# Three token blocks of 512 walked to and fro, and one addition of layer 1 done by accumulating DMAs

## The chip, the cores and the metric

The kernel runs on one core of one Trainium2 chip. The metric is the device time of one execution in microseconds. The kernel before takes 701.39 us (median of 3 runs, 701.15 to 702.93). TensorE (PE) multiplies; VectorE (DVE), ScalarE (ACT) and GpSimd (POOL) do the elementwise work; SyncE (SP) issues the DMAs.

## The reference

An attention block feeds two MLP layers, all in float32:

```python
scores = (1/8) * q @ k.T            # 2 batches, 8 heads, 768 positions, head_dim 64
keep   = (key < n_sink) | ((0 <= row - key) & (row - key < window))   # 4 sinks, window 128
x = softmax(scores where keep) @ v  # -> 1536 tokens x 512
h = x @ w_in                        # layer 1: 512 -> 2048
P = a0 + a1*h + a2*h^2 + a3*h^3
Q = 1 + |b0|*|h| + |b1|*h^2
x = (P / Q) @ w_out                 # 2048 -> 512
h = x @ w_in2                       # layer 2
out = (h * sigmoid(1.702*h)) @ w_out2
```

## The kernel before

**Tiling.** The 1536 tokens are cut into blocks (`TB`, line 31): 256, 384, 384 and 512 tokens, that is 2, 3, 3 and 4 query blocks of 128. The 2048 hidden columns are 16 tiles f of 128, in two halves of 8. A *unit* is one layer, one block and one half; `UNITS` (line 35) lists them layer by layer, half by half, block by block, so 8 units a layer. Every unit's result for a block is added to a partial sum `xf` that waits in SBUF until the block's second half comes.

**A piece.** Each unit is cut into pieces of up to 512 moving columns: one f for a block of 384 or 512 tokens, two f for the block of 256. A piece is a first product `h` (`g1`), the elementwise part (`el_a`, `el_b`) and a second product into `acc` (`g2`), which follows `LAG` = 3 pieces later. Every float32 factor is split into a high and a low float32r part, so each product is three matmuls: high x high, high x low, low x high. `g1` takes 4 row chunks x 3 = 12 matmuls for each f and block; `g2` in layer 1 takes 12 as well, with the block's tokens moving; `g2` in layer 2 takes 3 for each f and 128 tokens, with 512 weight columns moving.

**Elementwise, layer 1.** ACT writes `y` = |b0 h|, `z` (the square term, called sq) and `s`; DVE forms `s*h`, then `(s + a1)*h`, then `z = z + y` (line 713). ACT takes `r` = Ln(z), then Exp. DVE forms `gh` (the quotient), a correction in two steps (`z`, `s`), and `gl`, the low part. So DVE has seven operations a piece and ACT five. Layer 2 has two of each.

**Weights.** Every weight tile is loaded as int64 bits (`wraw`) and decoded once: ACT `dy`; DVE `dy`, `dt` and twice `dt<-wraw,dt`; then the high part (`wi` or `wo`, by ACT, DVE or POOL, whichever the planner picks), and the low part by DVE. There are 8 slots for each kind of weights, one more once attention is over, so a half's tiles can be decoded only as the half before it sets slots free.

**Attention** is done block by block: scores (PE, from `k` and `q`), masking with a running minimum `nm` (DVE `m`), Exp (ACT `a`), scaling by `rs` (`a<-a,rs`, POOL or DVE), transposes by `ident` (PE), copies `th` and `sT`, and the product with `vr` (PE). Layer 1 of a block needs all 8 heads of that block. While the first block's attention runs, PE gets filler matmuls (`acc<-zero`).

**What sets the order.** All operations are recorded and then ordered by a planner (`Program.play`): a list scheduler that prices every operation, picks the one with the longest tail plus a bias per category (`BIAS`), spaces the head pairs of attention (`HEAD`) and may hand an operation that several engines can do to another engine (`THETA`). Each engine then runs its list in exactly that order: an instruction that waits holds everything behind it on its engine. The profile gives the two lines of the planner's runner (L209 for matmuls and memsets, L210 for all else) for nearly all instructions, so groups are told apart by tile names.

The names in the steps that follow: pieces are counted from 0 in layer 1; `UNITS` (L35), `decode` (L605 on), `el_a`, `el_b`, `finish`, `attention`.

Of the kernel before, what the change touches and what calls it, by code (L numbers as in the profile page):

```python
# [6 lines left out]
F32R = mybir.dt.float32r  # L7
I32 = mybir.dt.int32
U32 = mybir.dt.uint32
AF = mybir.ActivationFunctionType  # L10
ALU = mybir.AluOpType
# [16 lines left out]
LN2_64 = 64.0 * 0.6931471805599453  # L28


TB = [[(0, [0, 1])], [(0, [2, 3, 4])], [(0, [5]), (1, [0, 1])], [(1, [2, 3, 4, 5])]]
XF_EARLY = (0, 1)

HALVES = [list(range(NF // 2)), list(range(NF // 2, NF))]
UNITS = [(m, T, fs) for m in (0, 1) for fs in HALVES for T in range(len(TB))]  # L35
GROUP = 3
LAG = 3

# [7 lines left out]
TH, SN, PE_OUT = "act/dve", "pool/dve", "act/dve"  # L46

BIAS = {
# [3 lines left out]
}  # L52
HEAD = (0.46, 1.43, 4.3, 7.1)
THETA = 1.27

WARM, FILL, FILL_AHEAD = 20, 6000, 0.1

# [4 lines left out]

START, PE_START, TICK, TICK_COLUMNS = 5.75, 6.25, 10.24 / 3, 3060
PE_LAT = 0.2
COL_FIX, COL_EACH = 0.4, 0.0275
TABLE = 1.3
LAT = 0.16
DMA_LAT, DMA_RATE, DMA_MIN = 1.9, 0.36e6, 65536


class View:
# [66 lines left out]
class Program:  # L138
# [56 lines left out]
    def op(self, eng, meth, alloc=(), alts=(), given=False, calls=(), cost=0.0, **kw):  # L195


        o = Op()
        o.i, o.eng, o.own = len(self.ops), eng, eng
        o.cat = self.cat  # L200
        o.table = 2 if kw.get("func") == AF.Sigmoid else 1 if kw.get("func") in (AF.Exp, AF.Ln) else 0
        views = [(k, v) for c in calls or [kw] for k, v in c.items() if isinstance(v, View)]

        def runner(eng, meth, kw):
            def run():
                a = {k: v.real() if isinstance(v, View) else v for k, v in kw.items()}
                e = getattr(self.nc, eng)
                if meth in ("matmul", "memset"):
                    return getattr(e, meth)(a.pop("out"), **a)  # L209
                return getattr(e, meth)(**a)  # L210
            return run
        o.lat = LAT
        o.nbytes = o.columns = 0
        if calls:
            runs = [runner(eng, meth, c) for c in calls]
            o.alts = {eng: (cost, lambda: [f() for f in runs][-1])}
            o.cost, o.lat = cost, PE_LAT
            o.columns = sum(c["rhs"].n * 4 * (c["lhsT"].box[0][1] - c["lhsT"].box[0][0]) / P for c in calls)
        elif eng == "sync":
            v = views[0][1]  # L220
            o.nbytes = (v.box[0][1] - v.box[0][0]) * v.n * 4
            o.cost, o.lat = 0.45 if v.box[0][1] - v.box[0][0] == P else 0.62, DMA_LAT
            o.alts = {eng: (o.cost, runner(eng, meth, kw))}
        else:
            self.columns = 0
            o.alts = {e: (self.price(e, m_, k_), runner(e, m_, k_)) for e, m_, k_ in [(eng, meth, kw)] + list(alts)}
            o.cost = min(c for c, _ in o.alts.values())
            o.columns = self.columns
            if eng == "tensor":
                o.lat = PE_LAT  # L230
        if given:
            o.alts, o.cost, o.lat, o.nbytes = {eng: (1e-6, lambda: None)}, 1e-6, given * 1.25 - 0.75, 0
        pre = {}
        for k, v in views:
            w = k in ("out", "accum_out")
            for q, box, wr in v.t.acc:
                if (w or wr) and overlap(box, v.box):
                    pre[q.i] = q
            if not v.t.acc:
                assert w, (v.t.name, k)  # L240
        o.allocs = [v.t for k, v in views if not v.t.acc] + [v.t for v in alloc if not v.t.acc]
        o.allocs = list(dict.fromkeys(o.allocs))
        o.begun = []
        for t in o.allocs:
            t.first = o
            t.acc.append((o, ((0, 0),), False))
        for t in dict.fromkeys([v.t for _, v in views] + [v.t for v in alloc]):
            if t not in o.allocs and not any(v.t is t for _, v in views):
                t.acc.append((o, ((0, 0),), False))
            if t.first is not o and t.first.i not in pre and (t.first.i, 0) not in pre:  # L250
                t.first.begun.append(o)
                pre[t.first.i, 0] = None
        for k, v in views:
            v.t.acc.append((o, v.box, k in ("out", "accum_out")))
        o.tiles = list(dict.fromkeys([v.t for _, v in views] + [v.t for v in alloc]))
        o.banks = [t for t in o.tiles if t.tag in PSUM_TAGS]
        o.preds = len(pre)
        o.succ = []
        o.next = []
        for q in pre.values():  # L260
            if q is not None:
                q.succ.append(o)
        o.ready = 0.0
        self.ops.append(o)
        return o
# [227 lines left out]
def emit(tc, qT, kX, vL, w_in, w_out, ca, cb, nw, out):  # L493
# [33 lines left out]
    def lo(eng, o, i, h):  # L527
        return tt(eng, ALU.subtract, o, i, h.bitcast(F32))

    cst_p = tc.tile_pool(name="cst", bufs=1)  # L530
    cst = cst_p.__enter__()
    SW = 2 * P + SC
# [72 lines left out]
    def decode(w, raw, dp, eng):  # L605

        lw, hw = raw[:, :, 0], raw[:, :, 1]
        y = R.tile(dp, [P, 512], F32, tag="dy", name="dy", bufs=2)
        t = R.tile(dp, [P, 512], I32, tag="dt", name="dt", bufs=2)
        R.op("scalar", "activation", out=y, in_=hw.bitcast(F32), func=AF.Abs)  # L610
        kw = dict(out=y, in0=y, scalar1=W_MIN, scalar2=W_MAX, op0=ALU.max, op1=ALU.min)
        R.op("vector", "tensor_scalar", **kw)
        kw = dict(out=t, in0=y.bitcast(I32), scalar1=0x07FFFFFF, scalar2=3, op0=ALU.bitwise_and, op1=ALU.logical_shift_left)
        R.op("vector", "tensor_scalar", **kw)
        R.op("vector", "scalar_tensor_tensor", out=t, in0=lw, scalar=29, in1=t, op0=ALU.logical_shift_right, op1=ALU.bitwise_or)
        R.op("vector", "scalar_tensor_tensor", out=t, in0=hw, scalar=-0x40000000, in1=t, op0=ALU.bitwise_and, op1=ALU.bitwise_or)
        hi(WH, w[:, 0, :], t.bitcast(F32))
        lo(eng, w[:, 1, :], t.bitcast(F32), w[:, 0, :])

    def moe(pools, blocks, units, x1_ready, late_pool):  # L620
# [80 lines left out]
        def el_a(i):  # L701
            m = steps[i][1]
            h = h_t.pop(i)[:, :wid(i)]
            if m == 0:
                y = R.tile(tp, [P, 512], F32, tag="y", name="y", bufs=2, more=(get_late, None, EL_MORE))[:, :wid(i)]
                s1 = R.tile(tp, [P, 512], F32, tag="s", name="s", bufs=2, more=(get_late, None, EL_MORE))[:, :wid(i)]
                z = R.tile(tp, [P, 512], F32, tag="z", name="z", bufs=2, more=(get_late, None, EL_MORE))[:, :wid(i)]
                R.op("scalar", "activation", out=y, in_=h, func=AF.Abs, scale=ab[:, 0:1])
                R.op("scalar", "activation", out=z, in_=h, func=AF.Square, scale=sb[:, 3:4])
                affine("act", s1, h, a_t[:, 3:4], a_t[:, 2:3])  # L710
                tt("dve", ALU.mult, s1, s1, h)
                R.op("vector", "scalar_tensor_tensor", out=s1, in0=s1, scalar=a_t[:, 1:2], in1=h, op0=ALU.add, op1=ALU.mult)
                tt("dve", ALU.add, z, z, y)
                el[i] = (z, s1)
            else:
                g = R.tile(tp, [P, 512], F32, tag="y", name="g", bufs=2, more=(get_late, None, EL_MORE))[:, :wid(i)]
                R.op("scalar", "activation", out=g, in_=h, func=AF.Sigmoid, scale=1.702)
                R.op("vector", "tensor_tensor", out=g, in0=g, in1=h, op=ALU.mult)
                el[i] = (g,)
# [108 lines left out]
    def build_banded():  # L828
        with (
# [22 lines left out]
            def attention(T, xs, alone):  # L852
# [74 lines left out]
                def scores(h):  # L927
# [9 lines left out]
                    for i, (b, qb) in enumerate(qs):  # L937
                        off, w = (P + SC, P) if qb == 0 else (0, 2 * P + SC)
                        k0 = kcol[b, max(0, qb - 1)] * KW
                        ps_ = [pst("s") for _ in t]  # L940
                        R.op("tensor", "matmul", alloc=[x for y in t for x in y[1:]], cost=w / 600 + 2 * COL_EACH, calls=[
                            dict(out=p[:, :w], lhsT=qr[r, i * P:(i + 1) * P], rhs=kr[r, k0:k0 + w], start=True, stop=True)
                            for p, (r, _, _, _) in zip(ps_, t)])
                        for p, (_, a, nm, sm) in zip(ps_, t):
# [48 lines left out]
                def values(h):  # L993
# [14 lines left out]
                    if sq:  # L1008
                        for e in (h, h + 1):
                            q0, n = qcol[sq[0]] * P, len(sq) * P  # L1010
                            calls.append(dict(out=x[(e % 2) * D:(e % 2 + 1) * D, q0:q0 + n], lhsT=vrs[e % 2][:SC, vcol[sq[0][0], "s"], :], rhs=st.pop(("sT", e))[:, :n], start=False, stop=True))
                    cost = COL_FIX + sum(c["rhs"].n / 1200 + COL_EACH for c in calls)
                    R.op("tensor", "matmul", calls=calls, cost=cost)
                    n, c = nq * P, h // 2
                    hi(XH, xs[0][c][:, :n], x[:, :n])
# [163 lines left out]
```

## Time and profile before

| what | value |
|---|---|
| median of 3 runs | 701.39 us |
| the profiled execution | 701.9 us |
| its span, first to last instruction | 700.1 us |
| PE busy | 670.2 us (96%) |
| DVE busy | 533.3 us (76%) |
| ACT busy | 407.2 us (58%) |
| POOL busy | 73.2 us (10%) |
| mean granted TensorE clock | 0.985 |

Busy shares are averages over the whole span. The 40-slice view shows DVE at 9 tenths in most slices up to about 420 us and at 1 to 8 tenths behind them, while PE stands at 9 nearly throughout. PE is pipelined: the mean time of one matmul is longer than the step from one to the next, which the chain of waits gives.

### The profile page before, as it was taken

How to read it: one execution, taken by the hardware profiler on the slowest of the kernel's cores; microseconds unless marked ns; L12 is line 12 of the kernel's file. 1: busy time of each engine (PE TensorE's matmuls, PEld its weight loads, DVE VectorE, ACT ScalarE, POOL GpSimd, SP SyncE). 2: the span in 40 equal slices, each digit the busy share in tenths (PEclk: the TensorE clock that was granted, in tenths of full speed). 3: DMA queues.
4: the chain of work that ended last, by engine and by line, in shares of the span. 5: the costliest groups of instructions: out<-in, count | busy, mean ns of one | idle time of the engine just before them, and what ended most of it. 6: DMA issues, size and time to landing. Idle time of an engine off the chain costs nothing.

```text
span 700.1 us, 10401 instructions
## 1 busy us (share of the span) xinstructions
PE 670.2 (96%) x3690; PEld 569.8 (81%) x3690; DVE 533.3 (76%) x1182; ACT 407.2 (58%) x894; POOL 73.2 (10%) x131
## 2 busy tenths in 40 slices
PE   8999989999999986799998999999999999999995
PEld 7677767877888865699997888988888898888874
DVE  7999899868759999999999999985278753222341
ACT  5899888967788665768585773543345432221220
POOL 4262452422200000000000000000000000000000
PEclk9999999999999997999999999999999999999999
DMA  5653554400001033300201011342023200000021
GB/s 170 212 171 109 157 156 137 154 26 1 24 0 31 31 118 111 106 27 8 84 0 32 1 58 63 121 141 70 1 91 120 91 31 16 0 16 1 15 76 65
DMA packets 26412, 49.75 MB, mean 71 GB/s; under 512 B 6384, under 2 KB 15088, under 8 KB 26352
## 3 DMA queue, kind: packets, MB, share of 16 engines
q1 hardware_dynamic: 26064, 49.00, 22.7%
q8 instruction: 31, 0.51, 0.3%
q14 instruction: 29, 0.24, 0.1%
q10 hardware_dynamic: 288, 0.00, 0.0%
HBM read 45.85 MB, written 3.15 MB: 70 GB/s over the span
## 4 chain that ended last, share of the span: by engine, by line
PE 82%; DVE 11%; ACT 3%; issue 1%; DMA 1%; POOL 1%; SPq 0%; DVEq 0%; POOLq 0%; ACTq 0%
PE att L209 32%; PE acc L209 25%; PE h L209 20%; PE att L210 3%; DVE dt L210 2%; DVE s L210 2%; DVE z L210 2%; PE acc L844 1%; DVE gh L210 1%; POOL a L210 1%; DVE dy L210 1%; DMA q<-q_t 1%; DVE wi L210 1%; DVE gl L210 1%; DVE m L210 1%
## 5 line engine op out<-in xcount | busy, mean ns | idle before, releaser
L209 PE MATMUL h<-xh,wi 128*128 128x384 f32 (+2 forms) x608 | 168.7, 342 | 7.2 <-DVE s L210 7.2
L209 PEld LDWEIGHTS h<-xh,wi 128*128 128x128 f32 x608 | 110.3, 193 | 21.7 <-DVE s L210 9.4
L209 PE MATMUL att<-xh,wi 128*128 128x384 f32 (+2 forms) x416 | 116.7, 343 | 0.6 <-DVE s L210 0.6
L209 PE MATMUL acc<-gh,wo 128*128 128x384 f32 (+2 forms) x384 | 105.7, 342 | 0.0
L209 PE MATMUL h<-xl,wi 128*128 128x384 f32 (+2 forms) x304 | 102.8, 338 | 0.0
L210 DVE TENSOR_TENSOR gl<-y,gh 128x384 fp32r<-128x384 f32 (+1 forms) x56 | 33.8, 613 | 82.1 <-PE acc L209 41.3
L209 PE MATMUL acc<-wo,gh 128*128 128x512 f32 x288 | 93.7, 395 | 0.0
L210 DVE SCALAR_TENSOR_TENSOR dt<-wraw,dt 128x512 int32<-128x512 int32 x128 | 89.0, 696 | 0.6
L209 PEld LDWEIGHTS att<-xh,wi 128*128 128x128 f32 x416 | 75.2, 188 | 7.6 <-DVE s L210 0.9
L210 ACT ACTIVATE gh<-y 128x384 fp32r<-128x384 f32 (+1 forms) x56 | 31.5, 569 | 75.9 <-PE acc L209 39.7
L209 PEld LDWEIGHTS acc<-gh,wo 128*128 128x128 f32 x384 | 69.2, 192 | 5.8 <-issue 2.0
L209 PE MATMUL att<-xl,wi 128*128 128x384 f32 (+2 forms) x208 | 71.4, 343 | 0.0
L210 POOL TENSOR_SCALAR a<-a,rs 128x272 f32<-128x272 f32 (+1 forms) x92 | 58.0, 647 | 109.2 <-DVE rs L210 71.8
L209 PE MATMUL acc<-gl,wo 128*128 128x384 f32 (+2 forms) x192 | 62.9, 341 | 5.9 <-DVE gl L210 5.9
L209 PEld LDWEIGHTS acc<-wo,gh 128*128 128x128 f32 x288 | 53.3, 188 | 10.4 <-ACT xf L210 0.4
L209 PEld LDWEIGHTS h<-xl,wi 128*128 128x128 f32 x304 | 58.7, 193 | 3.4 <-issue 0.4
L210 ACT ACTIVATE dy<-wraw 128x512 f32<-128x512 f32 x64 | 42.9, 670 | 25.8 <-DMA wraw<-w_out 14.1
L209 PE MATMUL acc<-wo,gl 128*128 128x512 f32 x144 | 52.7, 394 | 0.0
L210 ACT ACTIVATE a<-m,nm 128x272 f32<-128x272 f32 (+1 forms) x96 | 47.2, 493 | 5.5 <-DVE nm L210 4.7
L210 ACT ACTIVATE r<-z,ln_b 128x384 f32<-128x384 f32 (+1 forms) x56 | 37.0, 660 | 16.0 <-DVE z L210 15.8
L209 PEld LDWEIGHTS acc<-gl,wo 128*128 128x128 f32 x192 | 36.2, 192 | 10.1 <-DVE gl L210 7.8
L209 PE MATMUL att<-gh,wo 128*128 128x512 f32 (+2 forms) x128 | 40.8, 359 | 1.2 <-ACT xf L210 1.2
(118 smaller groups left out, 1234.4 us busy)
## 6 DMA issues: line engine op xcount, KB each, us to landing
wraw<-w_in SPq DMA_DIRECT2D x32, 512.0 KB, 3.6
wraw<-w_out SPq DMA_DIRECT2D x32, 512.0 KB, 3.5
out<-xf SPq DMA_DIRECT2D x12, 256.0 KB, 2.3
k<-k_x SPq DMA_DIRECT2D x12, 144.0 KB, 2.7
vr<-v_l SPq DMA_DIRECT2D x24, 64.0 KB, 2.5
k<-k_x SPq DMA_DIRECT2D x4, 360.0 KB, 3.6
vr<-v_l SPq DMA_DIRECT2D x8, 160.0 KB, 2.5
k<-k_x SPq DMA_DIRECT2D x4, 288.0 KB, 4.4
```

Source lines behind the costliest of these rows:

```text
L209: return getattr(e, meth)(a.pop("out"), **a)
L210: return getattr(e, meth)(**a)
L844: nc.tensor.matmul(R.real[k][:, 0:256], lhsT=zero[:, :P], rhs=zero, start=True, stop=True)
```

## The change

There are now three blocks of 512 tokens: batch 0's query blocks 0 to 3; its 4 and 5 with batch 1's 0 and 1; batch 1's 2 to 5. A piece is always one f and 512 columns: 48 pieces a layer, where there were 56 in layer 1 and 56 in layer 2. The units go to and fro: in layer 1 block 0 and block 1 with half 0, block 2 with both halves, block 1 and block 0 with half 1; in layer 2 block 2 and block 1 with half 0, block 0 with both halves, block 1 and block 2 with half 1. The block with both halves has no partial sum. In layer 1 `z = z + y` is a DMA from `y` to `z` that accumulates, issued by POOL. `dt` has three buffers, the planner's prices are new, and so are its tables (`BIAS`, `HEAD`, `THETA`). `add_minus` is defined and not called.

```diff
-TB = [[(0, [0, 1])], [(0, [2, 3, 4])], [(0, [5]), (1, [0, 1])], [(1, [2, 3, 4, 5])]]
-XF_EARLY = (0, 1)
+TB = [[(0, [0, 1, 2, 3])], [(0, [4, 5]), (1, [0, 1])], [(1, [2, 3, 4, 5])]]
+XF_EARLY = (0,)
-UNITS = [(m, T, fs) for m in (0, 1) for fs in HALVES for T in range(len(TB))]
+LAST = len(TB) - 1
+THERE, BACK = list(range(LAST)), list(range(LAST - 1, -1, -1))
+UNITS = ([(0, T, HALVES[0]) for T in THERE] + [(0, LAST, HALVES[0] + HALVES[1])] + [(0, T, HALVES[1]) for T in BACK]
+         + [(1, T, HALVES[0]) for T in [LAST] + BACK[:-1]] + [(1, 0, HALVES[0] + HALVES[1])] + [(1, T, HALVES[1]) for T in THERE[1:] + [LAST]])
...
-    "at0": 15.33, "at1": 21.93, "at2": 26.03, "at3": 6.7, "m0": -10.71, "m1": -2.77, "m2": -0.5,
+    "at0": 57.37, "at1": 40.94, "at2": -26.39, "at3": -86.3, "m0": -5.97, "m1": 87.68, "m2": 11.75,
...
-HEAD = (0.46, 1.43, 4.3, 7.1)
-THETA = 1.27
+HEAD = (5.08, 0.16, 15.06, 0.34)
+THETA = -0.68
...
-        elif eng == "sync":
+        elif meth == "dma_start":
...
+            if eng == "gpsimd":
+                o.nbytes *= 2
+                o.cost, o.lat = ADD_FIX, ADD_LAT + 0.6 * (kw["out"].dtype == F32R)
...
+    def add(out, in_):
+
+        R.op("gpsimd", "dma_start", out=out, in_=in_, accum_op=ALU.add)
...
-        t = R.tile(dp, [P, 512], I32, tag="dt", name="dt", bufs=2)
+        t = R.tile(dp, [P, 512], I32, tag="dt", name="dt", bufs=3)
...
-                tt("dve", ALU.add, z, z, y)
+                add(z, y)
```

**Where the first MLP matmul stands on PE.** `k,q` are scores, `th,vr` and `sT,vr` the products with v, `acc<-zero` fillers, `xh,wi` and `xl,wi` the first piece's `g1`. Before:

```order
L209 MATMUL h_324<-th_315,vr_200 64x256
L209 MATMUL h_324<-th_315,vr_200 64x128
L209 MATMUL att_294<-k_60,q_61 128x272
L209 MATMUL att_275<-k_60,q_61 128x272
L844 MATMUL acc_187<-zero 128x256 x5
L209 MATMUL att_322<-k_181,q_184 128x272
L209 MATMUL att_294<-k_181,q_184 128x272
L844 MATMUL acc_187<-zero 128x256
L209 MATMUL h_324<-xh_0_0_340,wi_302 128x256
L209 MATMUL h_324<-xl_0_0_348,wi_302 128x256
```

And of the change:

```order
L215 MATMUL h_432<-sT_386,vr_194 64x256
L215 MATMUL h_432<-sT_411,vr_198 64x256
L215 MATMUL att_359<-k_60,q_61 128x272
L215 MATMUL att_353<-k_60,q_61 128x272
L863 MATMUL acc_187<-zero 128x256 x6
L215 MATMUL h_432<-xh_0_0_459,wi_275 128x512
L215 MATMUL h_432<-xl_0_0_467,wi_275 128x512
L215 MATMUL att_357<-k_60,q_61 128x128
L215 MATMUL att_359<-k_60,q_61 128x128
```

Ahead of this row PE has 26 of the 96 score rows, 24 of 200 transposes, 16 of 144 products with v and 71 fillers before; of the change it has 40 of 96, 64 of 200, 40 of 136 and 130. Before its 25th MLP matmul the change has 56 scores, 96 transposes, 64 products and 153 fillers; the kernel before has as many scores, transposes and products (56, 92, 66) ahead of its 145th MLP matmul, with 110 fillers.

**ACT around the Ln of layer 1**, in the middle of the layer. `y`, `z`, `s` read the first product from PSUM (`h` or `att`), `r<-z` is the Ln, `r<-r` the Exp, `dy` and `wi` belong to the decoding. Before (the block of 512, first half):

```order
L210 ACTIVATE y_787<-h_324,ab 128x512
L210 ACTIVATE z_2341<-h_324,sb_179 128x512
L210 ACTIVATE r_691<-z_647,ln_b 128x512
L210 ACTIVATE s_2348<-h_324,a_t 128x512
L210 ACTIVATE dy_221<-wraw_64 128x512
L210 ACTIVATE wi_546<-dt_298 128x512
L210 ACTIVATE r_691<-r_691,ln_b 128x512
L210 ACTIVATE dy_243<-wraw_65 128x512
L210 ACTIVATE wi_611<-dt_239 128x512
L210 ACTIVATE y_2369<-att_275,ab 128x512
L210 ACTIVATE r_2358<-z_2341,ln_b 128x512
```

And of the change (block 2, both halves):

```order
L216 ACTIVATE y_933<-h_432,ab 128x512
L216 ACTIVATE z_961<-h_432,sb_179 128x512
L216 ACTIVATE s_976<-h_432,a_t 128x512
L216 ACTIVATE y_1062<-att_353,ab 128x512
L216 ACTIVATE z_2214<-att_353,sb_179 128x512
L216 ACTIVATE s_2219<-att_353,a_t 128x512
L216 ACTIVATE r_1001<-z_961,ln_b 128x512
L216 ACTIVATE r_1001<-r_1001,ln_b 128x512
L216 ACTIVATE r_2262<-z_2214,ln_b 128x512
L216 ACTIVATE r_2262<-r_2262,ln_b 128x512
L216 ACTIVATE dy_218<-wraw_64 128x512
```

Pieces now go through ACT in pairs, and each Ln, which waits for the accumulating DMA into its `z`, stands four instructions behind the one that wrote that `z`.

**Who does what.** Over the whole program, `a<-a,rs` on 272 columns stands 76 times on POOL and 4 times on DVE before, and 40 times on each of the change. The copies `th`, `sT` and `as` stand 3 times on DVE before and 38 times of the change. The high parts of the weights stand 6 times on POOL before and 27 times of the change, where POOL also issues the 48 DMAs.

## Rows read from the trace of the kernel before

**Rows 1.** The page's head and its busy times.

```profile
span 700.1 us, 10401 instructions
PE 670.2 (96%) x3690; PEld 569.8 (81%) x3690; DVE 533.3 (76%) x1182; ACT 407.2 (58%) x894; POOL 73.2 (10%) x131
```

**Rows 2.** Busy us by stretch: length, PE, PEld, DVE, ACT, POOL, clock, DMA.

```profile
36.00:91.00 55.00, 54.27 (x396) 41.66 (x395) 51.43 (x146) 49.65 (x149) 22.38 (x38) 1.00 0.49 141
91.00:212.00 121.00, 117.78 (x725) 95.29 (x724) 94.70 (x258) 94.75 (x253) 34.81 (x62) 0.99 0.23 69
212.00:300.00 88.00, 74.75 (x368) 63.58 (x367) 87.74 (x156) 59.97 (x100) 1.25 (x2) 0.93 0.27 84
300.00:410.00 110.00, 107.22 (x598) 100.64 (x598) 109.05 (x210) 77.49 (x136) 2.62 (x3) 1.00 0.07 20
410.00:693.00 283.00, 282.92 (x1400) 243.80 (x1398) 159.32 (x290) 100.12 (x184) 0.00 (x0) 1.00 0.18 56
```

**Rows 3.** Chain of waits, pieces from three windows: start, length, engine, tile, count.

```profile
283.84 0.42 DVE dt L210
...
284.86 0.60 DVE dt L210
...
293.54 0.66 DVE gh L210
...
484.87 2.08 PE att L209 x12
...
525.89 2.75 PE h L209 x12
...
556.76 2.87 PE h L209 x24
```

**Rows 4.** PE busy, 91 to 212 us, of tiles k, vr and ident in turn.

```profile
91.00:212.00 121.00, 14.11 (x80) 0.99 0.23 69
...
91.00:212.00 121.00, 24.67 (x156) 0.99 0.23 69
...
91.00:212.00 121.00, 18.01 (x108) 0.99 0.23 69
```

**Rows 5.** Groups by shape, DVE: name, shapes, count, busy us, mean ns, idle before.

```profile
L210 DVE TENSOR_TENSOR z<-z,y 128x384 f32<-128x384 f32 x32 | 18.3, 571 | 9.1 <-ACT z L210 9.1
...
L210 DVE TENSOR_TENSOR z<-z,y 128x512 f32<-128x512 f32 x24 | 16.3, 681 | 0.1
...
L210 DVE TENSOR_SCALAR a<-a,rs 128x272 f32<-128x272 f32 x4 | 1.6, 406 | 0.0
```

**Rows 6.** DMA issues: tiles, queue, count, KB each, median us to landing.

```profile
wraw<-w_in SPq DMA_DIRECT2D x32, 512.0 KB, 3.6
...
out<-xf SPq DMA_DIRECT2D x12, 256.0 KB, 2.3
...
q<-q_t SPq DMA_DIRECT2D x4, 192.0 KB, 4.5
```

**Rows 7.** Groups by shape, ACT on 512 columns.

```profile
L210 ACT ACTIVATE dy<-wraw 128x512 f32<-128x512 f32 x64 | 42.9, 670 | 25.8 <-DMA wraw<-w_out 14.1 <-DMA wraw<-w_in 11.6
...
L210 ACT ACTIVATE r<-r,ln_b 128x512 f32<-128x512 f32 x24 | 17.3, 721 | 0.4
...
L210 ACT ACTIVATE s<-h,a_t 128x512 f32<-128x512 f32 x15 | 11.6, 776 | 2.9 <-DVE gl L210 2.9
...
L210 ACT ACTIVATE y<-h,ab 128x512 f32<-128x512 f32 x15 | 10.3, 684 | 9.0 <-PE h L209 6.4 <-DVE dt L210 2.6
L210 ACT ACTIVATE z<-h,sb 128x512 f32<-128x512 f32 x15 | 10.2, 680 | 1.2 <-DVE s L210 1.2
```

**Rows 8.** Groups by shape, POOL.

```profile
L210 POOL TENSOR_SCALAR a<-a,rs 128x272 f32<-128x272 f32 x76 | 47.1, 635 | 76.7 <-DVE rs L210 44.6 <-ACT th L210 13.2 <-DVE nm L210 10.6
...
L598 POOL TENSOR_SCALAR mk<-mk 128x272 f32<-128x272 f32 x1 | 0.4, 419 | 0.2 <-DVE mk L596 0.2
```

**Rows 9.** Waits: engine, tile, releaser, us in total, times, longest.

```profile
POOL a L210 <- DVE rs L210: 71.8, 12, 21.1
```

More of the change, by code (lines that the diff above doesn't have):

```diff
@@ L64 @@
 PE_LAT = 0.2
-COL_FIX, COL_EACH = 0.4, 0.0275
+COL_EACH = 0.1
 TABLE = 1.3
@@ L68 @@
 DMA_LAT, DMA_RATE, DMA_MIN = 1.9, 0.36e6, 65536
+ADD_FIX, ADD_LAT = 0.9, 1.6
 class View:
@@ L528, in lo, with add_minus @@
         return tt(eng, ALU.subtract, o, i, h.bitcast(F32))
+    def add(out, in_):
+        R.op("gpsimd", "dma_start", out=out, in_=in_, accum_op=ALU.add)
+    def add_minus(o, i):
+        one_of([("gpsimd", "tensor_scalar", dict(out=o, in0=i, scalar1=-1.0, scalar2=0.0, op0=ALU.mult, op1=ALU.add)),
+                ("scalar", "activation", dict(out=o, in_=i, func=AF.Copy, scale=-1.0))])
+        add(o, i)
     cst_p = tc.tile_pool(name="cst", bufs=1)
@@ L940, in scores @@
                         ps_ = [pst("s") for _ in t]
-                        R.op("tensor", "matmul", alloc=[x for y in t for x in y[1:]], cost=w / 600 + 2 * COL_EACH, calls=[
+                        R.op("tensor", "matmul", alloc=[x for y in t for x in y[1:]], cost=w / 420 + 0.11, calls=[
                             dict(out=p[:, :w], lhsT=qr[r, i * P:(i + 1) * P], rhs=kr[r, k0:k0 + w], start=True, stop=True)
@@ L1011, in values @@
                             calls.append(dict(out=x[(e % 2) * D:(e % 2 + 1) * D, q0:q0 + n], lhsT=vrs[e % 2][:SC, vcol[sq[0][0], "s"], :], rhs=st.pop(("sT", e))[:, :n], start=False, stop=True))
-                    cost = COL_FIX + sum(c["rhs"].n / 1200 + COL_EACH for c in calls)
+                    cost = sum(c["rhs"].n / 1100 + COL_EACH for c in calls)
                     R.op("tensor", "matmul", calls=calls, cost=cost)
```

5 rows, old and new, of the table BIAS are left out of this document.

## The prediction

> **What bounds the kernel now.** The page's head gives the ratio of span to work: 700.1 us, PE busy for 96% of it, DVE for 76% [rows 1]. The profiled execution took 701.9 us, 1.8 more than its span and 0.5 more than the median of the runs shown; the sum below is made against the span, and these two are set right at the end. An average over the span hides which engine leads where, so the next view is busy time by stretch [rows 2]. From 36 to 91 us PE (54.3 of 55, part of it fillers) and DVE (51.4) are both near full. From 91 to 212 PE is full and DVE has room (94.7 of 121). From 212 to 410 DVE is full: 87.7 of 88 and 109.1 of 110, while PE loses 13.3 and 2.8 us and its clock falls to a mean of 0.93 in the first part. From 410 on PE alone is full.
>
> The step of one MLP matmul is read from the chain, where it is not blurred by pipelining [rows 3]: 2.87/24 = 0.1196 us with 256 columns, 2.08/12 = 0.1733 with 384, 2.75/12 = 0.2292 with 512. By the code there are 576, 1152 and 1152 of them, so 68.9 + 199.6 + 264.0 = 532.5 us.
>
> How much PE loses behind 91 us follows by subtraction. Ahead of that time stand, by the order, 144 MLP matmuls (132 with 256 columns, 12 with 384: 17.9 us), so 514.6 remain. Attention takes another 14.1 + 24.7 + 18.0 = 56.8 us there [rows 4]. That is 571.4 us of work in the 602 us up to 693: 30.6 are lost, 3.2 of them between 91 and 212. So the DVE-led stretch from 212 to 410 loses about 27 us, where the idle time alone shows 16; the rest is half clock and small gaps between matmuls.
>
> **The change, part by part.**
>
> *Fewer matmuls.* Three blocks of 512 need 2304 matmuls with 512 columns, 528.1 us instead of 532.5: −4.4. The columns are the same; only the fixed part of 576 matmuls goes. This lies on PE, which sets the end, so all of it counts.
>
> *The start.* Layer 1 can begin only when block 0's attention is through, and block 0 is now twice as large. I compare equal states. In the trace 80 of the 192 score records, two a row of the order, stand behind 91 us [rows 4]; so 56 of the 96 rows are done there, and 46% of the transposes. The changed order has the same ahead of its 25th MLP matmul, where the kernel before has done 144. At the same state, then, 17.9 − 24 × 0.2292 = 12.4 us of MLP work is missing. Is the state reached at the same time? DVE decides. Up to the second piece the order gives DVE as many decodes (14) as the kernel before has ahead of its fifth, about 3 pieces' elementwise work less (7 × 0.60 each, −12.6), 6 maskings less, 16 normalisations more (0.406 each [rows 5], +6.5) and 16 small copies more (no more than 0.42 each, a pass of DVE over 512 columns [rows 3], +5 to +7; the maskings at the same 0.42, −2.5). Net −2 to −4, and ACT and the fillers give nothing back, so the state comes at 91 to 95 us. I take +14; the bounds are +5 (PE picks matmuls up while it would have filled) and +22 (DVE waits on the longer chain of four score blocks a head).
>
> *The DVE-led stretch.* All 56 additions take 18.3 + 16.3 us by their own durations [rows 5]; at the chain's step, 0.60 where the mean of one is 0.68, some 30. About 36 of them lie between 212 and 410, 20 us. That leaves DVE 177 us of work there against 198 − 27 = 171 on PE: nearly even. The new order puts the heaviest part into block 2, which runs both halves at a stretch: 16 pieces and, by the order, 12 decodes. DVE needs 16 × (3 × 0.60 + 3 × 0.66) = 60.5 and 12 × (2 × 0.42 + 3 × 0.60) = 31.7, together 92.2 us; PE needs 16 × 24 × 0.2292 = 88.0. DVE leads by 4 there, and in the 16 pieces behind it (the way back, with few decodes) PE leads. So of 27 us some 21 come back. Bounds: 8, if DVE's heavier share of normalising (40 of 80 instead of 4) and copying is not done with when the stretch begins; 27, all of it.
>
> *The adds as DMAs.* POOL issues 48; what they cost is how long a Ln waits. ACT stands in order: behind a Ln that waits are the Exp of its piece, the next `y`, `z`, `s`, and so the PSUM banks of the next first products. The trace has no accumulating DMA. The nearest are 256 KB in 2.3 us and 512 KB in 3.6; the slowest is 4.5 [rows 6]. An accumulate reads two tiles of 256 KB and writes one, so I take 3.6, with bounds 2.3 and 4.5, plus what POOL is late. In the new order `s`, the next `y` and `z`, and `s` again stand between a `z` and its Ln: 0.776 + 0.684 + 0.680 + 0.776 = 2.9 us [rows 7]. A pair of pieces takes ACT 2 × (0.684 + 0.680 + 0.776 + 2 × 0.721) = 7.2 us and, with 18 decode steps and copies for block 2's 16 pieces at about 0.65, 8.6. PE needs 11.0 for a pair. So ACT can wait 2.4 us a pair, and an add costs nothing until it takes 2.9 + 2.4 = 5.3 us; each microsecond beyond costs 24 pairs × 1 = 24 us. At 3.6 the cost is 0. Below nothing it can't be: the Ln gets no earlier than after DVE's 0.68.
>
> GpSimd's own operations are slower beside a busy DVE: 0.635 us for 272 columns where the one on the quiet chip took 0.419 [rows 8]. The Trainium skill, page "SBUF — State Buffer", section "🔬 SBUF: two separate sides", has the rule behind it and against this change: GpSimd writes the descriptors of its DMAs through a port pair that a VectorE operation in a two-port mode holds for its whole length, so such DMAs wait. By that page's example (620 ns alone, about 3100 beside a copy) an add would take, as an estimate, 2.5 us more, and the sum would be some 19 us higher. I go by the row: 0.2 us a time, and 3.6 + 0.2 stays well under 5.3.
>
> *No cost taken:* the partial sums (one block fewer a layer, on ACT and DVE beside PE), the first units of layer 2 (they take block 2, whose input is ready long before), the end (four chunks of 512 as now).
>
> The sum: −4.4 + 14 − 21 + 0 = −11.4. From the profiled execution 701.9 − 11.4 = 690.5, less 0.5 to the median: 690 us.
>
> **Rivals.**
>
> *The adds are late.* Place: the Ln of layer 1 on ACT; it decides from 5.3 us on. For it: POOL is in order, and its queue in the attention phase waited 71.8 us in 12 waits for `rs`, 21.1 at the longest [rows 9]; an add behind such a normalisation waits as well, and rows 8 show POOL slowed by DVE. Against: no landing over 4.5 us, and behind attention POOL has only copies ahead of the adds. At 6.5 us an add, 1.2 × 24 = 29 us: 690 + 29 = 719. Slower.
>
> *The start takes what the stretch gives.* If the doubled first block costs 22 us and only 12 come back, −4.4 + 22 − 12 = +6; with the middle of either, 0. For it: DVE has 51.4 of 55 us filled in the start, and gets half of POOL's normalising. Against: equal work by the count above. About 701, no change that can be told.
>
> *All of it comes back.* If decodes spread evenly over layer 1 and the start costs 6: −4.4 + 6 − 27 = −25, 676 us. For it: DVE's total falls by more than PE's; against: the slots bind half 1's decodes to block 2.
>
> **How the numbers follow.** Forecast 0.46 (its own range 680 to 698), late adds 0.21, eaten by the start 0.16, all back 0.17. A measurement of this kernel tells about 0.3% (2 us) from no change. Faster are the forecast, the last case and a quarter of the third: 0.67; same 0.11; slower the late adds and a few of the third: 0.22. To leave 2 in 10 out, the range runs from 674, under the last case, to 707, the beginning of the late adds.
>
> **What would show it.** The first MLP matmul near 60 us instead of 36, and about 92 us at the 25th. PE idle between some 220 and 310 us down from 13 to under 5. DVE's total near 500 us. ACT's waits at `r<-z` for DMAs under 2.4 us a pair; if they come to more, and PE waits for ACT or for `gl`, the adds are late and the forecast is wrong. If PE is full from 91 us on and the time still is 700, the start was mis-sized.

## The result, and the profile after

The changed kernel takes 694.14 us (median of 4 runs, 693.83 to 695.05) where the kernel before took 701.27 (4 runs beside them): ratio 0.9891, 95% interval 0.9863 to 0.9918. That is 7.1 us less; 690 was predicted, within 674 to 707.

The page's head and its busy times, to be set against [rows 1]:

```profile
span 692.9 us, 9131 instructions
PE 670.3 (97%) x3141; PEld 518.0 (75%) x3141; DVE 518.8 (75%) x1101; ACT 380.0 (55%) x786; POOL 102.2 (15%) x144
```

PE's busy time is the same; the span is 7.2 us shorter. DVE lost 14.5 us, not the 34.6 of the additions. The stretches of [rows 2] (length, PE, PEld, DVE, ACT, POOL, clock, DMA):

```profile
36.00:91.00 55.00, 53.62 (x343) 37.15 (x342) 52.63 (x171) 43.07 (x131) 21.14 (x29) 1.00 0.63 179
91.00:212.00 121.00, 118.95 (x613) 83.31 (x611) 101.92 (x265) 90.36 (x223) 25.72 (x39) 1.00 0.37 88
212.00:300.00 88.00, 86.69 (x383) 68.15 (x382) 82.02 (x136) 59.44 (x98) 20.36 (x25) 1.00 0.42 89
300.00:410.00 110.00, 104.19 (x440) 82.82 (x440) 103.26 (x171) 73.99 (x117) 19.93 (x23) 0.98 0.42 92
410.00:693.00 283.00, 274.31 (x1190) 221.97 (x1188) 153.16 (x261) 93.66 (x159) 3.60 (x4) 0.99 0.20 60
```

From 212 to 300 us PE's idle time falls from 13.3 to 1.3 us and the clock is back at 1.00; from 300 to 410 it grows from 2.8 to 5.8. (1.00 is the upper of TensorE's two clock levels, 2.4 GHz; 0.50 would be the lower, 1.2 GHz; what lies between is a mean over both.) Where did the crowd of 260 to 300 go? DVE's busy time on the decoding tile `dt` alone, first the kernel before, then the changed one:

```profile
212.00:260.00 48.00, 13.97 (x23) 1.00 0.18 55
260.00:300.00 40.00, 19.31 (x33) 0.84 0.38 119
300.00:410.00 110.00, 9.75 (x16) 1.00 0.07 20
```

```profile
212.00:260.00 48.00, 13.17 (x21) 1.00 0.42 89
260.00:300.00 40.00, 8.48 (x13) 1.00 0.42 89
300.00:410.00 110.00, 23.78 (x40) 0.98 0.42 92
```

Before, 33 decoding passes fell into 40 us, and there the clock's mean was 0.84. Now 13 do, and 40 come behind 300 instead of 16.

**The balance.** PE's busy time of `xh` ahead of 91 us, then `k`, `vr` and `ident` behind it, in the changed kernel:

```profile
0.00:91.00 91.00, 6.39 (x16) 0.94 0.59 176
...
91.00:693.00 602.00, 15.01 (x84) 0.99 0.30 76
...
91.00:693.00 602.00, 24.39 (x154) 0.99 0.30 76
...
91.00:693.00 602.00, 16.78 (x104) 0.99 0.30 76
```

16 products with `xh`, two in three of a group, make 24 MLP matmuls ahead of 91 us. Behind it stand 2304 − 24 = 2280 at 0.2292, 522.6 us, and 56.2 of attention: 578.8. PE's last matmul ends at 684.7, so 593.7 − 578.8 = 14.9 us are lost. Before, it ended at 692.9: 601.9 − 571.4 = 30.5. So the work behind 91 grew by 7.4 (+11.8 for the start, −4.4 for fewer matmuls), 15.6 fewer are lost, and the end behind the last matmul is 1.0 longer (8.2 for 7.2): −7.2, the difference of the spans. These 11.8 hold 12.4 of MLP work not yet done at 91 us and 0.6 less attention behind it.

**The adds.** The logarithm by shape, the add's tile, and its DMA (KB each, median us to landing), three views of the changed kernel:

```profile
L216 ACT ACTIVATE r<-z,ln_b 128x512 f32<-128x512 f32 x48 | 34.6, 722 | 33.5 <-DMA z<-y 33.4
```

```profile
L216 POOL DMA_DIRECT2D z<-y x48: 852/872/1167, 79.2 to 404.9; - x48
...
DMA to landing us min/median/max: 3.3/3.3/6.4
```

```profile
z<-y POOLq DMA_DIRECT2D x48, 256.0 KB, 3.3
```

An add takes POOL 0.87 us and lands 3.3 us from its issue in the median, under the 3.6 taken; still the 48 logarithms waited 33.4 us in all. The median hides a tail: followed one by one in the trace, 18 of the 48 adds landed later than 3.6 us, nine later than 4.5 and four only after 5.4 to 6.4. Behind those 18 stand 23.7 of the 33.4 us. Of the 26 adds that had DMAs of other tiles on their way beside them (between an add's issue and 3.3 us later) 14 were among the late ones, of the other 22 four; this is a coincidence in time, and what delays an add is not shown.

What such a wait does is seen in the chain of waits (start, length, what), in two places; the add at 251.68 took 4.57 us:

```profile
251.68 4.57 DMA z<-y
256.27 0.73 ACT r L216
257.03 0.72 ACT r L216
257.75 0.58 ACT z L216
258.33 0.56 ACT dy L216
258.92 0.82 DVE dy L216
259.74 0.59 DVE s L216
260.40 0.87 issue
261.27 0.74 DVE s L216
262.06 1.43 PE h L215 x5
...
319.65 6.29 DMA z<-y
325.97 0.73 ACT r L216
```

The first of these adds ends late, ACT stands at the logarithm, behind it the next `z` and a decode's `dy`, DVE waits for that `dy`, and `s` behind it holds PE's next first products: the delay goes from one engine's list to the next until it reaches PE.

### The profile page after: what moved, and what is told of

The parts are those of the page before. It is cut to its first block, busy times and chain, and to the rows that moved or that the text cites. A ratio compares the mean times of both kernels' runs of the same rounds, so it can differ in the third digit from the quotient of the medians.

```text
span 692.9 us, 9131 instructions
## 1 busy us (share of the span) xinstructions
PE 670.3 (97%) x3141; PEld 518.0 (75%) x3141; DVE 518.8 (75%) x1101; ACT 380.0 (55%) x786; POOL 102.2 (15%) x144
## 3 DMA queue, kind: packets, MB, share of 16 engines
q0 software_dynamic: 6912, 12.59, 10.8%
## 4 chain that ended last, share of the span: by engine, by line
PE 75%; DVE 7%; issue 6%; ACT 5%; DMA 5%; POOL 1%; SPq 0%; DVEq 0%; POOLq 0%; ACTq 0%
PE att L215 26%; PE acc L215 24%; PE h L215 19%; DMA z<-y 3%; PE att L216 3%; PE acc L863 2%; DVE s L216 2%; DVE dt L216 1%; ACT th L216 1%; DVE gl L216 1%; DMA q<-q_t 1%; ACT r L216 1%; DVE z L216 1%; ACT a L216 1%; ACT sT L216 1%
## 5 line engine op out<-in xcount | busy, mean ns | idle before, releaser
L215 PE MATMUL h<-xh,wi 128*128 128x512 f32 x448 | 151.5, 396 | 2.2 <-DVE s L216 1.7
L215 PE MATMUL att<-xh,wi 128*128 128x512 f32 x320 | 106.7, 391 | 0.0
L215 PE MATMUL acc<-gh,wo 128*128 128x512 f32 x288 | 100.6, 404 | 3.3 <-ACT wo L216 2.2
L215 PE MATMUL h<-xl,wi 128*128 128x512 f32 x224 | 88.0, 393 | 0.0
L216 DVE TENSOR_TENSOR gl<-y,gh 128x512 fp32r<-128x512 f32 x48 | 32.8, 689 | 66.7 <-PE acc L215 54.9
L216 POOL DMA_DIRECT2D z<-y x48 | 42.3, 887 | 192.5 <-ACT z L216 175.1
L215 PE MATMUL att<-xl,wi 128*128 128x512 f32 x160 | 62.5, 391 | 0.0
L216 ACT ACTIVATE dy<-wraw 128x512 f32<-128x512 f32 x64 | 42.9, 671 | 29.7 <-DMA wraw<-w_out 19.6
L215 PE MATMUL acc<-gl,wo 128*128 128x512 f32 x144 | 55.5, 403 | 1.5 <-DVE gl L216 1.4
L216 ACT ACTIVATE r<-z,ln_b 128x512 f32<-128x512 f32 x48 | 34.6, 722 | 33.5 <-DMA z<-y 33.4
L215 PE MATMUL att<-wo,gh 128*128 128x512 f32 x128 | 47.6, 396 | 0.4 <-POOL wo L216 0.3
L216 DVE SCALAR_TENSOR_TENSOR gh<-s,a_t,r 128x512 fp32r<-128x512 f32 x48 | 36.0, 751 | 11.5 <-ACT r L216 10.5
```

## The experiments

The ratio of each is to executions of the kernel before beside it, whose medians were 701.27 to 702.53 us; so a difference under 1 us between two rows tells nothing. "Lost" is worked out as in the balance above, from each run's own rows: end of PE − 91 − 522.6 − attention behind 91 (24 MLP matmuls stand ahead of 91 us in each kernel with the new blocks).

| run | blocks, walk, add | us | ratio [95% interval] | PE ends, attention | lost |
|---|---|---|---|---|---|
| the change | new, new, DMA | 694.14 | 0.9891 [0.9863, 0.9918] | 684.7, 56.2 | 14.9 |
| add_on_dve | new, new, DVE | 706.53 | 1.0072 [1.0054, 1.0089] | 696.4, 54.6 | 28.2 |
| new_blocks_old_walk | new, old, DMA | 703.74 | 1.0028 [1.0012, 1.0044] | 695.8, 55.4 | 26.8 |
| old_blocks_new_walk | old, new, DMA | 708.34 | 1.0079 [1.0055, 1.0103] | | |
| old_blocks_dma_add | old, old, DMA | 702.08 | 1.0017 [1.0004, 1.0030] | | |
| old_blocks_add_64_columns | the same, adds cut | 696.20 | 0.9915 [0.9900, 0.9930] | | |
| add_64_columns | the change, adds cut | 686.92 | 0.9790 [0.9771, 0.9810] | 675.6, 54.3 | 7.7 |
| short_dve_op | the change, one DVE pass cut | 687.71 | 0.9793 [0.9773, 0.9813] | 678.4, 55.2 | 9.6 |
| both_cuts | both of these | 683.32 | 0.9739 [0.9724, 0.9753] | 673.0, 54.7 | 4.8 |
| add_priced_later | the change, other price | 694.17 | 0.9886 [0.9867, 0.9905] | | |
| more_y_and_z | the change, more buffers | 695.56 | 0.9901 [0.9882, 0.9921] | | |
| low_parts_by_dma | the change, less DVE | 701.21 | 0.9979 [0.9959, 0.9998] | | |
| late_low_parts_by_dma | the same, 16 tiles | 697.29 | 0.9935 [0.9914, 0.9956] | | |

### Which part carries the gain: add_on_dve, old_blocks_dma_add

```diff
-                add(z, y)
+                tt("dve", ALU.add, z, z, y)
```

> The changed kernel with z = z + y back on VectorE; the planner orders it anew. Theory A (the stretch from 212 to 410 us gave back 13 instead of 21 us because each Ln waits for its accumulating DMA): the waits of ACT at r<-z for DMAs, 33 us in 22 waits, go; VectorE gets 30 us more work, so the two nearly cancel: 692 to 702. Theory B (VectorE still leads in block 2 and the DMA's latency is hidden): 30 us more on the leading engine, some 20 of them in the stretch, 708 to 718.

Measured: 706.53 us, slower than the kernel before, and between the ranges of the two theories. Busy time from 212 to 410 us (columns as above):

```profile
212.00:300.00 88.00, 85.34 (x378) 65.93 (x377) 81.53 (x134) 58.30 (x98) 2.96 (x4) 1.00 0.12 33
300.00:410.00 110.00, 99.80 (x421) 79.81 (x420) 106.79 (x179) 74.60 (x119) 3.61 (x4) 0.95 0.15 47
```

With the additions DVE is at 106.8 of 110 behind 300 us and PE loses 10.2 there. Without the adds as DMAs the rest of the change gives back 2.3 us of the 30.5 (28.2 are lost), while the work behind 91 us grows by 5.8 (522.6 + 54.6 − 571.4): the adds as DMAs are worth 12.4 us there, the new order of work that comes with them included.

The other half alone, the kernel before with its add as a DMA:

```diff
-                tt("dve", ALU.add, z, z, y)
+                R.op("gpsimd", "dma_start", out=z, in_=y, accum_op=ALU.add)
```

> The kernel before (four blocks, old walk, its own tables) with the addition as an accumulating DMA, priced as in the change. VectorE loses 30 us, about 20 in the stretch that it leads. Theory B and the prediction's third step: 681 to 689 (12 to 20 us under 701). Theory A: the Ln waits take most of it, 694 to 702.

Measured: 702.08 us, no gain, at the upper end of theory A's range. Taking some 25 us off DVE brings nothing in the old blocks. Each half alone is worth nothing or less, together 7 us. Two things stand against reading this as the adds and the blocks alone. Each of the two kernels was planned anew with tables found for another kernel. And the third `dt` buffer, the new prices and the new tables went with the new blocks; no run has them in the old ones.

### Blocks or walk: new_blocks_old_walk, old_blocks_new_walk

```diff
+UNITS = [(m, T, fs) for m in (0, 1) for fs in HALVES for T in range(len(TB))]
```

> The change, with its three blocks of 512 and its adds as DMAs, but each half of a layer goes through the blocks 0, 1, 2 in the old order instead of to and fro; the order of work is planned anew. In the change block 2 has its two halves at a stretch, 16 pieces beside which the decoding of the weights falls on DVE. Theory A (the walk is what spreads DVE's work; without it DVE leads again in half 0 and PE waits): 700 us or more, PE's idle time between 212 and 410 us again at 10 us and more, the ratio to the kernel before not under 0.997. Theory B (blocks of 512 with the adds off DVE are enough, the walk adds little): 692 to 696, ratio 0.987 to 0.993.

> The four old blocks (256, 384, 384, 512) with the adds as DMAs and the new walk to and fro; the order of work is planned anew. With the old walk and the same adds the time was 702.1. Theory A (the walk carries the gain): 694 to 697. Theory B (the width of the pieces does: in a piece of 256 or 384 columns PE has 24 x 0.1196 = 2.9 or 24 x 0.1733 = 4.2 us of work, and an add's 0.4 us to its issue and 3.0 to 3.4 to its landing don't fit beside it): 700 to 704, ACT's waits at the logarithms for the adds 25 us or more in all.

Measured: 703.74 and 708.34. In the first, theory A held: the new blocks without the walk lose 26.8 us, though less in the place expected (PE's idle time from 212 to 410 is 9.4). In the second both theories are off, the walk does harm in the old blocks. Each kernel kept the planner's tables of its blocks, found for another walk; how much of the loss is that, stays open. DVE's `dt` from 260 to 300 us, in old_blocks_new_walk 26 passes, in new_blocks_old_walk:

```profile
212.00:260.00 48.00, 7.06 (x11) 1.00 0.34 66
260.00:300.00 40.00, 11.68 (x20) 1.00 0.44 99
300.00:410.00 110.00, 28.69 (x47) 1.00 0.46 101
```

The new blocks already end the crowd of 33; the old walk puts more of the decoding behind 300 us (47 against 40 in the change).

### What the adds cost: add_64_columns, old_blocks_add_64_columns

```diff
-        R.op("gpsimd", "dma_start", out=out, in_=in_, accum_op=ALU.add)
+        R.op("gpsimd", "dma_start", out=out[:, :64], in_=in_[:, :64], accum_op=ALU.add)
```

> The changed kernel, same order on every engine, each accumulating DMA moves only 64 of the 512 columns, so z lacks y in 448 columns (that part of the addition is left out). Only the DMA's length changes. Theory A: from issue to landing about 2.2 instead of 3.3 us, waits at r<-z down from 33 to under 15 us, time 684 to 689. Theory B: 692 to 694.5, the waits shorter and nothing gained.

Measured: 686.92 us, 7.2 less than the change with the same order on every engine. The DMA lands in 2.2 us instead of 3.3 (medians; 5 of the 48 take over 3.6 us instead of 18), and ACT's waits fall from 33.4 us in 22 to (waits: engine, tile, releaser, total, times, longest)

```profile
ACT r L216 <- DMA z<-y: 12.6, 8, 2.7
```

So 20.8 us less waiting on ACT are 7.2 us of the time, about a third. The cut also moves an eighth of the bytes; that it is the time to landing and not the traffic is inferred from the waits.

> The kernel before with the adds as DMAs, in the same order as in the run of 702.1, where each add moves 64 columns of its piece; the addition is left out in the other columns. In the change this cut took 7.2 us off. Theory A (the adds' time to landing is what eats the gain in the short pieces of the old blocks): 56 adds in pieces of 2.9 to 5.5 us of PE, so more than in the change: 690 to 694, ACT's waits at the logarithms down from 27.8 us to under 12. Theory B (the old blocks lose their gain elsewhere: PE has 4.4 us more of work there, and the decoding and the pieces fall together on DVE): 698 to 702.

Measured: 696.20, between the theories: 5.9 us by the medians (7.2 by the ratios) from the adds' time to landing, no more than in the change. ACT's waits fell to 10.1 us, as theory A said, but its larger gain did not come: the width of the pieces is not shown to be why the old blocks gain nothing. Their `dt` on DVE shows what is left:

```profile
260.00:300.00 40.00, 20.30 (x34) 0.87 0.38 110
```

The crowd of decoding at 260 to 300 us is still there, 34 passes and a low clock, whatever the adds cost.

### What DVE still costs: short_dve_op, both_cuts

The correction's subtraction of layer 1 on 64 of 512 columns, the order unchanged (`price` keeps the planner's cost):

```diff
-  R.op("vector", "scalar_tensor_tensor", out=s1, in0=s1, scalar=a_t[:, 0:1], in1=z, ...)
+  R.op("vector", "scalar_tensor_tensor", out=s1[:, :64], in0=s1[:, :64], scalar=a_t[:, 0:1], in1=z[:, :64], ...)
```

> The changed kernel, same order on every engine, one of VectorE's six operations a piece in layer 1 (s<-s,a_t,z) works on 64 of 512 columns (the rest of that correction is left out): 0.6 us less on VectorE in each of 48 pieces, 29 us in all, 17 in the stretch. Theory B: 682 to 687. Theory A: 691 to 694, since Ln still waits for the DMA.

Measured: 687.71, 6.4 less, 0.7 above the range of theory B. The group went from 744 to 296 ns:

```profile
L216 DVE SCALAR_TENSOR_TENSOR s<-s,a_t,z 128x64 f32<-128x64 f32 x48 | 14.1, 296 | 0.2
```

21.5 us off DVE give 6.4, with the waits for the adds as long as before (32.3 us).

> The change in its own order on all engines with both cuts at a time: each add moves 64 of its 512 columns and DVE's subtraction s<-s,a_t,z of layer 1 is made on 64 of 512 (addition and correction are left out in the other columns). Alone the first took 7.2 us off 694.1, the second 6.4. Theory A (two separate losses: some pieces wait for the add, others for DVE): 694.1 - 7.2 - 6.4 = 680.5, at most 682. Theory B (one chain, add, logarithm, exponential, DVE's product, in which either cut gives the same slack): 685 to 687.

Measured: 683.32, 10.8 less than the change, between the sum of the two (13.6) and the larger (7.2), so between the two theories: partly two losses, partly one chain. What remains is 4.8 us, and PE is busy for 196.9 of the 198 us:

```profile
212.00:300.00 88.00, 87.75 (x389) 69.89 (x388) 79.38 (x143) 59.97 (x95) 19.34 (x24) 1.00 0.23 54
300.00:410.00 110.00, 109.17 (x472) 87.88 (x471) 101.12 (x182) 76.69 (x122) 20.35 (x23) 1.00 0.24 58
```

### Can it be had: add_priced_later, more_y_and_z

```diff
-ADD_FIX, ADD_LAT = 0.9, 1.6
+ADD_FIX, ADD_LAT = 0.9, 2.8
```

> The change with one number of the planner altered: an add is taken to be through 0.9 + 2.8 us after its turn on GpSimd instead of 0.9 + 1.6, near the 3.7 us and more from z's end to the logarithm in the trace of the change; the order is planned anew. Theory A (the change's order sets the logarithms too early because the add's price is too low; with the measured price the wait is filled): ACT's waits at the logarithms fall from 33.4 us to under 20, time 688 to 692. Theory B (what the add takes must be paid somewhere: at two pieces in flight no order has work enough to put in between, and the tables were found for the other price): the waits move to another place, 694 to 702.

```diff
-  y = R.tile(..., bufs=2, more=(get_late, None, EL_MORE))     # y, z and g
+  y = R.tile(..., bufs=2, more=(get_late, None, EL_MORE + 1))
```

> The change with one more buffer each for y and z in layer 1 once attention is through, planned anew, the add's price as in the change. Theory A (the adds' latency can't be hidden because only so many pieces may be in flight): with one more piece in flight ACT waits less, 688 to 692. Theory B (the latency is not seen by the plan, or what is in flight is bounded by the three pieces between first and second product): 693 to 698, the waits at the logarithms near 33 us.

Measured: 694.17 and 695.56, no better than the change. The waits at the logarithms did fall, the more with the buffers, first add_priced_later and then more_y_and_z:

```profile
ACT r L216 <- DMA z<-y: 23.8, 15, 4.0
```

```profile
ACT r L216 <- DMA z<-y: 15.0, 16, 4.4
```

The times are those of theory B in both; its reason holds for the price alone, since with the buffers the waits did fall by half. A wait taken away by another order is not one taken away by a shorter add: PE is idle from 212 to 410 us for 9.2 us (add_priced_later) and 8.5 (more_y_and_z), where the change has 7.1. With more buffers over half of it is one wait for a weight's high part, which ACT makes:

```profile
PE att L215 <- ACT wi L216: 4.8, 1, 4.8
```

In the change no single wait of PE in this stretch is over 1.7 us.

### Less DVE by more DMAs: low_parts_by_dma, late_low_parts_by_dma

```diff
-        lo(eng, w[:, 1, :], t.bitcast(F32), w[:, 0, :])
+        add_minus(w[:, 1, :], t.bitcast(F32))
```

The second run does this only for layer 1's second half (`m == 0 and f in HALVES[1]`).

> The change, and the low parts of the 64 decoded weight tiles (wi<-dt,wi and wo<-dt,wo, on DVE 21.8 + 21.8 = 43.6 us) are made without DVE: GpSimd or ACT writes the negated, rounded value and an accumulating DMA adds the unrounded one; planned anew. These DMAs have time, since a weight tile is used long after. Theory A (DVE's load still costs some 6 us: cutting it by 20 us in the change's own order gave 6.4): DVE near 475 us, time 684 to 689. Theory B (GpSimd takes all in order; 64 negations of 0.7 us and 64 issues of 0.9 us more, about 100 us, stand ahead of the adds that the logarithms wait for, and dt's buffers stay taken for 4 us longer): ACT's waits at the logarithms grow beyond 45 us, time 696 to 706.

> The change, with only the 16 weight tiles of layer 1's second half (decoded behind the start, beside block 2) getting their low part by a negation on GpSimd or ACT and an accumulating DMA; planned anew. In the run with all 64 the DMA engines were busy for 0.81 to 0.85 of 36 to 91 us (0.61 to 0.64 in the change), and the z adds took 3.8 us to their landing instead of 3.3. Theory A (the start and the crowded queue ate what DVE gained there; 16 tiles take 16 x 0.68 = 11 us off DVE just where it leads): 688 to 692. Theory B (each DMA added behind an add in GpSimd's order and on the DMA engines gives back through the adds what DVE gains): 694 to 699, the adds' landing again at 3.6 us and more.

Measured: 701.21 and 697.29; neither gains, they are 7.1 and 3.2 us slower than the change. Theory B was right that nothing comes back, its place was wrong in the first: ACT's waits at the logarithms are 32.8 us, not over 45. What changed is the DMA. First the start of low_parts_by_dma (the DMA engines' share is 0.83, in the change 0.63), then its landings, then the add's landing in late_low_parts_by_dma:

```profile
36.00:91.00 55.00, 52.90 (x326) 36.30 (x325) 49.19 (x158) 43.15 (x126) 27.66 (x42) 0.97 0.83 210
```

```profile
z<-y POOLq DMA_DIRECT2D x48, 256.0 KB, 3.8
wi<-dt POOLq DMA_DIRECT2D x32, 256.0 KB, 4.4
```

```profile
z<-y POOLq DMA_DIRECT2D x48, 256.0 KB, 3.5
```

DVE's total fell by 23.9 us in the first and by 2.4 in the second, where longer passes took back part (`gh<-s,a_t,r` 834 ns in the mean, 751 in the change). With 16 tiles the landing is 3.5, under the 3.6 that theory B named. Which share of the loss is DMA traffic, GpSimd's queue or the new order is open.

## Why the prediction was right, point by point

The direction and the place were right, and the mechanism but for the price of the adds; the time is 4 us above the forecast. That is −2.2 from the start, −1.8 from the stretch with free adds, +7.2 from the adds and +1.0 from the end behind the last matmul, which was put at nothing. So the closeness of the time owes a little to errors of two signs.

- **Fewer matmuls, −4.4.** The chain of the changed kernel has the same step (12 matmuls in 2.72 to 2.80 us behind 410 us), so the term follows from the counts; it was not tested alone.
- **The start, +14.** Measured +11.8: at 91 us 24 MLP matmuls are done, the 25th begins within 2.5 us of it, and 84 score records stand behind it where 80 did [rows 4]. The state came at 91, the lower of the 91 to 95 predicted. The first MLP matmul began at 66.4, not near 60; the state at 91 us came as predicted all the same.
- **The stretch, −21.** −15.6 for all behind 91 us with the adds as they are, and −15.6 − 7.2 = −22.8 with short ones: this term had the right size if the adds were free. It rested on DVE leading PE by only 4 us in block 2, so on the additions being off DVE; add_on_dve shows that with them 2 us come back. PE's idle time from 220 to 310 us fell from 13.3 to 2.8, under the 5 named beforehand.
- **The adds, 0: the step that failed.** Measured at least 7.2 us, what add_64_columns gives back; its adds still take 2.2 us. Two things are off in the step. It took one duration for all adds. The median was right (3.3 to landing against 3.6), but four adds took longer than the 5.3 us up to which an add was to be free. By the step's own rule those four would cost 0.11 + 0.99 + 1.12 + 1.12 = 3.3 us, so the larger part lies in the rule. The logarithm waits 33.4/24 = 1.4 us a pair, under the 2.4 that were to be free, and yet the adds cost: the sign that was named for free adds came out and was no proof of them. The 2.4 were ACT's mean slack over a pair. ACT's list is fixed, and in a piece where DVE decodes too a wait goes through ACT to DVE and PE, as the chain at 251.68 us shows; of the 20.8 us of waiting that the short adds took away, a third was time.
- **DVE's total near 500.** 518.8. It left out what the change gives to DVE: 49 normalisations `a<-a,rs` of 19.6 us instead of 4 of 1.6, about as much as the gap. 29 of them lie between 106 and 201 us, where DVE had room, the other 20 ahead of 91 us; the term for the start had counted 16.
- **GpSimd beside a busy DVE.** The issue took POOL 852 to 1167 ns, and 33 of the 48 adds lie between 212 and 410 us, where DVE is busy for 185.3 of 198. By the prediction's estimate from the Trainium skill, page "SBUF — State Buffer", section "🔬 SBUF: two separate sides", an add would have taken 2.5 us more than 3.6, that is 6.1. For most adds the trace does not show that: 30 of 48 landed within 3.6 us. Three took 6.3 to 6.4; whether a VectorE operation held GpSimd up there, or another DMA did, no run here shows. What did grow is POOL's own `a<-a,rs`: 736 ns where it took 635 [rows 8].

**The rivals.** *Late adds, 719:* its mechanism is there at a quarter of its price (7.2 us for 29). It took 6.5 us for every add; the median is 3.3, and only three came near it (6.3, 6.4 and 6.4). *The start eats the gain:* 11.8 and not 22. *All comes back:* on the stretch both_cuts, with a loss of 4.8, is about that case, and needs work left out.

## What to carry to other kernels

Here DVE's load had to be cut and its work spread: either alone, as planned here, brought nothing, so test the parts of such a change together as well as singly. Moving a pass to a DMA is not free because the mean slack covers its median latency. Look at the longest landings, not the median alone, and count the pieces in which the waiting engine's list holds up the engine that leads; in this kernel a third of the wait that shorter adds removed was time. The next pass moved the same way can cost more than it frees, as both runs with the low parts did.

## What the runs showed of the hardware

An accumulating DMA within SBUF, issued by GpSimd, has a time to landing that grows far less than its size: 32 KB 2.2 us (add_64_columns), 192 KB 3.0 (old_blocks_dma_add), 256 KB 3.3 (the change; medians). Single ones are far off the median: in the change the longest took 6.4 us. With 16 and 64 more such DMAs in the kernel the same 256 KB took 3.5 and 3.8 in the median, and with 64 those into `wi` 4.4.

Single DVE passes are long where GpSimd works beside them. In late_low_parts_by_dma the pass `gh<-s,a_t,r` took at most 756 ns in the 36 pieces where no elementwise operation of GpSimd ran beside it; of the 12 others eight took 1095 to 2406 ns. The longest, and what GpSimd did meanwhile (start, length):

```profile
304.82 2.41 DVE L216 SCALAR_TENSOR_TENSOR gh<-s,a_t,r 128x512 fp32r<-128x512 f32 x1
```

```profile
304.58 0.86 POOL L216 DMA_DIRECT2D z<-y  x1 [2.87 <-ACT z L216]
305.16 1.52 POOL L216 TENSOR_SCALAR wi<-dt 128x512 fp32r<-128x512 f32 x2
```

The granted clock between 260 and 300 us (columns of the stretches) before and after:

```profile
260.00:300.00 40.00, 27.54 (x150) 24.13 (x151) 39.85 (x73) 26.66 (x46) 0.00 (x0) 0.84 0.38 119
```

```profile
260.00:300.00 40.00, 39.06 (x168) 30.84 (x167) 39.55 (x65) 25.90 (x40) 9.21 (x11) 1.00 0.42 89
```

DVE is as full in both. Before, PE waited for it, and the clock fell to the lower of its two levels (0.50, 1.2 GHz), as two rows of the kernel before show; after, it stays at the upper one (1.00, 2.4 GHz):

```profile
272.00:276.00 4.00, 0.10 (x1) 0.10 (x1) 4.00 (x9) 2.64 (x5) 0.00 (x0) 0.67 0.43 131
276.00:280.00 4.00, 4.00 (x19) 4.00 (x20) 4.00 (x8) 1.32 (x2) 0.00 (x0) 0.50 0.26 74
```

PE stood idle for most of the first four microseconds and ran the next four at the lower level. So a part of what the change gave back is that clock; how large a part was not measured by itself.
